# A hash-bucketed attention and two MoE blocks on one core: the order of the attention's queues, chosen anew

## The chip, the cores and the metric

The kernel runs on one core of a Trainium2 chip. The metric is the device time of one execution in microseconds; before the change the median of three runs is 786.19. The engines are TensorE (PE, with its weight loads as PEld), VectorE (DVE), ScalarE (ACT), GpSimd (POOL) and SyncE (SP), which issues all DMAs. Each engine works through its own queue in the order of the program, and an instruction that waits holds all that stand behind it.

## The reference

Sixteen heads (2 batches of 8) of 768 positions and width 64, then two feed-forward blocks over the 1536 tokens of width 512. Cut to what matters:

```python
q_bits = (einsum('bhsd,dk->bhsk', q, proj) > 0)           # six bits; k_bits likewise
mask = bucket(q_bits)[:, :, :, None] == bucket(k_bits)[:, :, None, :]
scores = where(mask, scale * q @ k.T, -1e9)
attn = exp(scores - max(scores)); attn = attn / (sum(attn) + 1e-9)
x = (attn @ v)                                            # [1536, 512]
h = x @ w_in; g = (a0 + a1*h + a2*h2 + a3*h3) / (1 + |b0||h| + |b1|h2 + 1e-6); x = g @ w_out
h = x @ w_in2; out = (h - tanh(h)) @ w_out2
```

## The kernel before

The attention goes head by head, and the heads overlap. For each head h, `load_qk` fetches keys and queries (`kq`), `split_hi` (ScalarE) and `split_lo` (GpSimd) make a rounded part `A` and a rest `Bl`, and `place` copies them by DMA into the operand tiles `TA`, `TBk` and `TBq`. `bits` multiplies with the projection on TensorE, and VectorE turns the signs into mask rows of `TBk` (L361). `smax` (L376) makes the masks' products and VectorE takes each row's maximum `mx` (L380), six blocks j of 128 positions to a head; `put_max` transposes the maxima on TensorE (`mt`, L391), and VectorE makes `mr` of them (L396), which goes to a row of `TBq` by DMA. `scores` (L498) then makes the block `st` of scores, ScalarE its exponential `e` (L501); the exponential is rounded to `eh` by ScalarE (L507), in blocks 2 and 4 partly by VectorE (L509), GpSimd makes the rest `el` (L518), and `attend` multiplies both with V into `pv` (18 small matmuls to a block).

V is read once for a pair of heads (`vraw`). Its scale is a chain through two engines: `vmax` (VectorE, `vm`, L420), `vall` (transpose on TensorE, L429), `vback` (VectorE, L433 and L434, the last writes `vdg`), `vagain` (TensorE, L437) and `vscale` (VectorE, L447 to L450, writes `vsc`). With it `vhi` (ScalarE, L469) and `vlo` (VectorE, L473) write the two halves of the tile `VB`; `vmean_of` (L480) sums over V on TensorE, and ScalarE and VectorE bring that to `VM` (L485, L486). `normalize` (VectorE, L549 to L552) and `to_x` (TensorE transposes, `xh` on ScalarE, `xl` on VectorE, L576) end a pair of heads.

PSUM is shared out in three double banks "d" (for `sm`, `st`, `bits`, `xT`, and the first MoE products `hr`), taken in turn, and one single bank "s" for `mt`, `vt` and the sum over V. A matmul into "d" waits for whoever read the tile three places earlier.

The order is written by hand, by a table. Each step is put on a list with a place: the head's number times six plus an entry of the table `T` (or of `EARLY` for heads 0 to 3, or `T_LAST`), and the list is sorted:

```python
on(g + j, scores, h, j)
on(g + j + T["exp"], out_of, "e", (h, j))
on(g + j + T["round"], round_e, h, j)
on(g + T["vlo"], vlo, h)
...
for _, _, fn, args in sorted(tasks, key=lambda x: x[:2]):
    fn(*args)
```

So a number of the table has no time of its own: it only decides what stands ahead of what on each engine. `EH_ACT_LAST` and `EL_DVE_LAST` say how much of the last head's rounding each engine does. Behind the attention stand the two MoE blocks, whose order is another table, `M`.

Of the kernel before, what the change touches and what calls it, by code (L numbers as in the profile page):

```python
# [38 lines left out]


T = dict(load=-22.01, hi=-15.34, lo=-14.2, place=-13.97, place_a=-13.59, bits=-13.42, bits_out=-12.57,
         put=-3.25, put_out=-3.12, vhi=-6.87, vlo=-4.93, vmean=-2.03, vmean_out=-1.18, lead=9.98, max=0.3,
         exp=0.13, round=0.9, rest=1.95, pv=(5.43, 6.95, 7.43, 8.75, 8.06, 9.23), pv_last=(5.5, 5.5, 7.19,
         8.17, 8.91, 9.32), norm=9.74, x=14.29, x_out=15.02, v=-16.67, vmax=-11.5, vall=-10.2, vscale=-9.9,
         w=-24, w_step=3.88, h0=0.75, slot=0.88, a=0.84, b=2.13, c=2.55, d=4.03, e=4.18, gates=26.99,
         vback=-10.1, vagain=-9.93, w2=-8.0, w2_step=4.0, w_load=6.0)
EARLY = {0: dict(load=-61, hi=-59.04, lo=-59.03, place=-57.89, bits=-57.11, bits_out=-56.82, place_a=-56.45,
                lead=54.43, put=-49.1, v=-59.99, vmax=-57.43, vall=-55.7, vscale=-55.6, vhi=-4.1, vlo=-4.02,
                vmean=-2.21, vmean_out=-1.2, vback=-55.67, vagain=-55.64, put_half=-51.0),
         1: dict(load=-66.5, hi=-64.64, lo=-64.4, place=-61.82, bits=-59.23, bits_out=-58.61, place_a=-57.18,  # L50
                lead=53.53),
         2: dict(load=-64.71, hi=-60, lo=-59.75, place=-59.59, place_a=-59.53, bits=-56.42, bits_out=-56.02,
                lead=9.98, v=-22.32),
         3: dict(load=-20, hi=-15.31, lo=-14.17, place=-14.21, place_a=-13.68, bits=-12.43, bits_out=-11.41,
                lead=9.23)}
NE = 1
T_LAST = dict(norm=9.59, x=10.17, x_out=10.68)
# [3 lines left out]
def tile_fn(ctx: ExitStack, tc: tile.TileContext, kq, v, proj, w1i, w1o, a_, b_, w2i, w2o, out):  # L61
# [180 lines left out]
    with ExitStack() as actx:  # L242
# [354 lines left out]
        for h in range(BH):  # L597
            g, last = 6 * h, h == BH - 1
            T = {**TT, **EARLY.get(h, {})}
            if h > 0:  # L600
# [190 lines left out]
```

## Time and profile before

| | |
|---|---|
| median of three runs | 786.19 us (782.45 to 789.70) |
| profiled execution | 783.02 us, span 781.2 us |
| TensorE busy in the span | 745.8 us (95%) |
| VectorE, ScalarE, GpSimd busy | 525.8, 466.2, 507.0 us (67%, 60%, 65%) |
| attention | up to some 264 us of the span |
| MoE blocks | from there to the end |

A row of the time line names the start in us from the span's start, the duration, the engine, the line of the program, the operation and its operands, and in brackets how long the engine stood idle just before and who ended that. Buffer numbers are left out of the names, so `mx` is the tile of any head.

### The profile page before, as it was taken

How to read it: one execution, taken by the hardware profiler on the slowest of the kernel's cores; microseconds unless marked ns; L12 is line 12 of the kernel's file. 1: busy time of each engine (PE TensorE's matmuls, PEld its weight loads, DVE VectorE, ACT ScalarE, POOL GpSimd, SP SyncE). 2: the span in 40 equal slices, each digit the busy share in tenths (PEclk: the TensorE clock that was granted, in tenths of full speed). 3: DMA queues.
4: the chain of work that ended last, by engine and by line, in shares of the span. 5: the costliest groups of instructions: out<-in, count | busy, mean ns of one | idle time of the engine just before them, and what ended most of it. 6: DMA issues, size and time to landing. Idle time of an engine off the chain costs nothing.

```text
span 781.2 us, 13222 instructions
## 1 busy us (share of the span) xinstructions
PE 745.8 (95%) x5081; PEld 627.9 (80%) x5081; DVE 525.8 (67%) x820; ACT 466.2 (60%) x756; POOL 507.0 (65%) x395
## 2 busy tenths in 40 slices
PE   4799999999899699999999999999999999999998
PEld 3689888888787588888888888888888888888886
DVE  6678988898879888879899898853322444342222
ACT  2388888878796788777666676764444333332120
POOL 2298898988889687787777778985333434342221
PEclk9999999999999999999999999999999999999999
DMA  6564546447421231121222211221221212200012
GB/s 169 159 164 129 136 135 166 127 112 193 119 77 61 62 101 55 55 80 56 59 76 76 61 54 56 74 86 55 71 64 55 82 54 60 77 27 1 28 41 95
DMA packets 40536, 66.49 MB, mean 85 GB/s; under 512 B 3844, under 2 KB 26468, under 8 KB 40472
## 3 DMA queue, kind: packets, MB, share of 16 engines
q1 hardware_dynamic: 40472, 65.63, 28.8%
q8 instruction: 40, 0.66, 0.4%
q14 instruction: 24, 0.20, 0.1%
HBM read 43.00 MB, written 3.15 MB: 59 GB/s over the span
## 4 chain that ended last, share of the span: by engine, by line
PE 82%; DVE 12%; ACT 2%; issue 2%; DMA 1%; SPq 0%; ACTq 0%; DVEq 0%
PE h L171 32%; PE y L691 17%; PE y L687 17%; PE st L498 6%; DVE mx L380 4%; PE sm L376 3%; PE bits L352 2%; DVE eh L509 1%; PE pv L536 1%; DVE VB L473 1%; PE pv L537 1%; PE pv L539 1%; DVE TBk L361 1%; ACT e L501 1%; DMA vraw<-in_v_dram 1%
## 5 line engine op out<-in xcount | busy, mean ns | idle before, releaser
L239 POOL TENSOR_TENSOR G<-g,G 128x512 fp32r<-128x512 f32 x96 | 123.4, 1295 | 119.5 <-ACT G L234 104.6
L518 POOL TENSOR_TENSOR el<-e,eh 128x768 f16<-128x768 f32 (+2 forms) x96 | 159.1, 1673 | 33.0 <-ACT eh L507 20.2
L171 PE MATMUL h<-xh,wh 128*128 128x512 f32 x368 | 144.0, 391 | 3.6 <-DVE wt L110 3.6
L171 PE MATMUL h<-xl,wh 128*128 128x512 f32 x368 | 143.7, 390 | 0.0
L171 PE MATMUL h<-xh,wl 128*128 128x512 f32 x368 | 143.7, 390 | 0.0
L122 POOL TENSOR_TENSOR wl<-wt,wh 128x512 fp32r<-128x512 f32 x64 | 83.6, 1306 | 71.7 <-ACT wh L121 71.1
L687 PE MATMUL y<-G,wh 128*128 128x512 f32 x384 | 118.3, 389 | 0.0
L691 PE MATMUL y<-wh,G 128*128 128x512 f32 x384 | 118.1, 389 | 0.0
L234 ACT CAST G<-g 128x512 fp32r<-128x512 f32 x96 | 58.3, 619 | 84.9 <-PE y L691 35.7
L501 ACT ACTIVATE e<-st,lnk 128x768 f32<-128x768 f32 x96 | 86.2, 899 | 31.7 <-PE st L498 28.3
L110 DVE SCALAR_TENSOR_TENSOR wt<-wt,low 128x512 int32<-128x512 int32 x64 | 44.0, 687 | 89.5 <-ACT wt L98 85.2
L704 DVE TENSOR_TENSOR ya<-y,ya 128x512 f32<-128x512 f32 x72 | 49.1, 688 | 77.8 <-PE y L691 72.7
L380 DVE TENSOR_REDUCE mx<-sm 128x1 f32<-128x768 f32 x96 | 90.7, 951 | 12.7 <-PE sm L376 10.7
L171 PEld LDWEIGHTS h<-xh,wh 128*128 128x128 f32 x368 | 69.5, 189 | 18.2 <-issue 3.8
L691 PEld LDWEIGHTS y<-wh,G 128*128 128x128 f32 x384 | 72.1, 188 | 14.9
L687 PEld LDWEIGHTS y<-G,wh 128*128 128x128 f32 x384 | 72.1, 188 | 14.9
L209 ACT ACTIVATE s<-h 128x512 f32<-128x512 f32 x48 | 28.5, 598 | 90.4 <-PE h L171 90.3
L171 PEld LDWEIGHTS h<-xh,wl 128*128 128x128 f32 x368 | 69.4, 188 | 14.6
L171 PEld LDWEIGHTS h<-xl,wh 128*128 128x128 f32 x368 | 69.5, 189 | 14.4
L691 PE MATMUL y<-wl,G 128*128 128x512 f32 x192 | 74.7, 389 | 0.0
L687 PE MATMUL y<-G,wl 128*128 128x512 f32 x192 | 74.7, 389 | 0.0
L507 ACT CAST eh<-e 128x768 f16<-128x768 f32 (+2 forms) x92 | 68.1, 740 | 1.5
(122 smaller groups left out, 1603.2 us busy)
## 6 DMA issues: line engine op xcount, KB each, us to landing
raw<-in_w1i_dram SPq DMA_DIRECT2D x16, 512.0 KB
raw<-in_w1o_dram SPq DMA_DIRECT2D x16, 512.0 KB
raw<-in_w2i_dram SPq DMA_DIRECT2D x16, 512.0 KB
raw<-in_w2o_dram SPq DMA_DIRECT2D x16, 512.0 KB
kq<-in_kq_dram SPq DMA_DIRECT2D x16, 384.0 KB
TA<-A SPq DMA_DIRECT2D x32, 192.0 KB
TA<-Bl SPq DMA_DIRECT2D x32, 192.0 KB
vraw<-in_v_dram SPq DMA_DIRECT2D x8, 384.0 KB
```

The lines of the kernel that those rows point to most:

```text
L122: lo_eng.tensor_sub(lo, w, hi)
L171: nc.tensor.matmul(ps, l[:, dc], r[:, dc], start=(n == 0), stop=(n == 11))
L234: nc.scalar.copy(gh, live[u, fi])
L239: nc.gpsimd.tensor_sub(gl, live.pop((u, fi)), gt[u, fi])
L380: d = nc.vector.tensor_reduce(mx[h][:, j:j + 1], ps, axis=AX.XY, op=ALU.max)
L498: nc.tensor.matmul(ps[:, n], l[h][0:k, j * P:(j + 1) * P], q[h][0:k, n * SH:(n + 1) * SH], start=(k == P), stop=(k < P))
L501: outs["e", (h, j)] = lambda: nc.scalar.activation(halved(e), ps, AF.Exp, scale=1.0 / math.sqrt(D), bias=lnk)
L507: nc.scalar.copy(eh[h, j][:, 0:n], ef[h, j][:, 0:n])
L518: nc.gpsimd.tensor_sub(el[h, j][:, n:S], e[:, n:S], eh[h, j][:, n:S])
L687: nc.tensor.matmul(ps, l[:, o], r, start=(n == 0), stop=(n == 11))
L691: nc.tensor.matmul(ps, l[:, o], r, start=(n == 0), stop=(n == 11))
L704: nc.vector.tensor_add(ya, ps, ya)
```

## The change

Only the tables `T` and `EARLY` have other numbers. `M`, `T_LAST`, `EH_ACT_LAST` and `EL_DVE_LAST` are as they were. The core of the diff:

```diff
-         put=-3.25, put_out=-3.12, vhi=-6.87, vlo=-4.93, vmean=-2.03, vmean_out=-1.18, lead=9.98, max=0.3,
-         exp=0.13, round=0.9, rest=1.95, pv=(5.43, 6.95, 7.43, 8.75, 8.06, 9.23), pv_last=(5.5, 5.5, 7.19,
...
+         put=-3.25, put_out=-3.08, vhi=-6.87, vlo=-3.9, vmean=-1.86, vmean_out=-0.71, lead=9.98, max=0.3,
+         exp=0.42, round=0.9, rest=1.95, pv=(5.43, 6.95, 7.92, 8.75, 8.16, 9.23), pv_last=(5.5, 5.5, 7.99,
```

VectorE's queue in the middle of the attention, where heads 8 and 9 overlap; `mx9` are maxima of head 9, `vt5`, `vdg5` and `vsc5` the scale of the sixth pair, `VB0` the low half of V for head 9. Before:

```order
L380 TENSOR_REDUCE mx9_2173<-sm9_4_2374 128x1
L420 TENSOR_REDUCE vm5_2379<-vraw5_2141 128x2
L473 SCALAR_TENSOR_TENSOR VB0_124<-vraw4_1599,vsc4_1933,VB0_124 128x6x64
L380 TENSOR_REDUCE mx9_2173<-sm9_5_2409 128x1
L433 TENSOR_REDUCE vt5_2433<-vt5_2433 2x1
L434 TENSOR_TENSOR vdg5_2435<-ident_64,vt5_2433 2x2
L447 TENSOR_SCALAR vt5_2433<-vt5_2433 128x2
L448 TENSOR_SCALAR vt5_2433<-vt5_2433 128x2
L450 RECIPROCAL vsc5_2475<-vt5_2433 128x2
L380 TENSOR_REDUCE mx10_2450<-sm10_0_2451 128x1
L396 TENSOR_SCALAR mr9_0_2502<-mt9_0_2500 6x128
L509 CAST eh8_2_2505<-e8_2_2444 128x384
```

And with the change:

```order
L420 TENSOR_REDUCE vm5_2377<-vraw5_2139 128x2
L380 TENSOR_REDUCE mx9_2172<-sm9_4_2374 128x1
L380 TENSOR_REDUCE mx9_2172<-sm9_5_2409 128x1
L433 TENSOR_REDUCE vt5_2412<-vt5_2412 2x1
L434 TENSOR_TENSOR vdg5_2414<-ident_64,vt5_2412 2x2
L473 SCALAR_TENSOR_TENSOR VB0_124<-vraw4_1597,vsc4_1915,VB0_124 128x6x64
L447 TENSOR_SCALAR vt5_2412<-vt5_2412 128x2
L448 TENSOR_SCALAR vt5_2412<-vt5_2412 128x2
L450 RECIPROCAL vsc5_2457<-vt5_2412 128x2
L380 TENSOR_REDUCE mx10_2449<-sm10_0_2450 128x1
L509 CAST eh8_2_2502<-e8_2_2443 128x384
L396 TENSOR_SCALAR mr9_0_2505<-mt9_0_2500 6x128
```

`vm5` has gone ahead of a maximum, `VB0` from ahead of `vdg5` to behind it, and the cast of `eh8_2` ahead of `mr9`. The last of these moves is there in every head.

ScalarE's queue at the end of head 8 (`e8_4` and `e8_5` are exponentials, `VB1` the high half of V for head 10, `VM0` the sum over V of head 9). Before:

```order
L501 ACTIVATE e8_4_2561<-st8_4_2562,lnk_70 128x768
L485 ACTIVATE VM0_134<-vm9_2548 64x64
L507 CAST eh8_4_2590<-e8_4_2561 128x512
L501 ACTIVATE e8_5_2595<-st8_5_2596,lnk_70 128x768
L469 ACTIVATE VB1_125<-vraw5_2141,vsc5_2475 128x6x64
```

And with the change:

```order
L501 ACTIVATE e8_4_2548<-st8_4_2549,lnk_70 128x768
L507 CAST eh8_4_2588<-e8_4_2548 128x512
L469 ACTIVATE VB1_125<-vraw5_2139,vsc5_2457 128x6x64
L485 ACTIVATE VM0_134<-vm9_2562 64x64
L501 ACTIVATE e8_5_2593<-st8_5_2594,lnk_70 128x768
```

`VM0` has gone behind `eh8_4`, and `VB1` ahead of `e8_5`. VectorE's part of `VM` (L486) has gone behind its cast of `eh` in block 4 likewise.

SP's queue at the start of the program, before:

```order
L280 DMA kq0_96<-in_kq_dram 128x768
L286 DMA praw_95<-in_proj_dram 128x6
L280 DMA kq1_140<-in_kq_dram 128x768
L415 DMA vraw0_142<-in_v_dram 128x6x128
L335 DMA TBk0_153<-A0_144 64x768
L336 DMA TBq0_154<-A0_144 64x768
L342 DMA TA0_152<-A0_144 64x768 x2
L342 DMA TA0_152<-Bl0_145 64x768 x2
L335 DMA TBk1_173<-A1_148 64x768
```

And with the change:

```order
L280 DMA kq0_96<-in_kq_dram 128x768
L286 DMA praw_95<-in_proj_dram 128x6
L415 DMA vraw0_140<-in_v_dram 128x6x128
L280 DMA kq1_142<-in_kq_dram 128x768
L335 DMA TBk0_153<-A0_144 64x768
L336 DMA TBq0_154<-A0_144 64x768
L335 DMA TBk1_169<-A1_148 64x768
L336 DMA TBq1_170<-A1_148 64x768
L342 DMA TA0_152<-A0_144 64x768 x2
L342 DMA TA0_152<-Bl0_145 64x768 x2
```

`vraw0` has gone ahead of `kq1`, and the copies of head 1's `A1` ahead of four copies of head 0. On TensorE, `vall` and `vagain` of most pairs have each gone ahead of one block of pv, and the sum over V (L480) behind the next scores or `smax`; the first `smax` of head 1 stands ahead of the second half put of head 0, and in the last head the product `hr0_1` stands ahead of a pv block.

## Rows read from the trace of the kernel before

**Rows 1.** Stretches: start and end, length, busy us and instructions by engine, TensorE's granted clock, DMA

```profile
130.00:157.00 27.00, 25.74 (x349) 23.04 (x347) 23.52 (x39) 22.19 (x32) 23.75 (x15) 1.00 0.51 136
184.00:211.00 27.00, 24.13 (x286) 20.13 (x286) 24.21 (x39) 20.12 (x30) 21.65 (x15) 0.94 0.57 148
...
264.00:510.00 246.00, 245.51 (x1077) 203.23 (x1078) 214.65 (x322) 175.64 (x302) 195.12 (x171) 0.99 0.22 69
```

**Rows 2.** TensorE's waits from 50 to 186 us: total, times, longest

```profile
PE vt L437 <- DVE vdg L434: 3.5, 4, 0.9
PE bits L352 <- DVE mx L380: 0.7, 3, 0.3
...
PEld sm L376 <- DVE xl L576: 0.8, 2, 0.4
```

**Rows 3.** Time line of VectorE around the scale of a pair

```profile
137.55 0.96 DVE L380 TENSOR_REDUCE mx<-sm 128x1 f32<-128x768 f32 x1
...
139.41 1.67 DVE L473 SCALAR_TENSOR_TENSOR VB<-vraw,vsc,VB 128x384 f16<-128x384 f32 x1
141.01 0.94 DVE L380 TENSOR_REDUCE mx<-sm 128x1 f32<-128x768 f32 x1
...
142.19 0.14 DVE L434 TENSOR_TENSOR vdg<-ident,vt 2x2 f32<-2x2 f32 x1
142.80 0.17 DVE L447 TENSOR_SCALAR vt<-vt 128x2 int32<-128x2 int32 x1 [0.47 <-PE vt L437]
...
143.21 0.17 DVE L450 RECIPROCAL vsc<-vt 128x2 f32<-128x2 f32 x1
```

**Rows 4.** Time line of TensorE at the same place

```profile
142.39 0.38 PE L437 MATMUL vt<-vdg,pj 2*128 2x2 f32 x2 [0.94 <-DVE vdg L434]
...
143.43 0.27 PE L391 MATMUL mt<-ident,mx 128*6 128x128 f32 x1
```

**Rows 5.** Instructions on VB, 30 to 240 us: shortest, median, longest in ns

```profile
L473 DVE SCALAR_TENSOR_TENSOR VB<-vraw,vsc,VB x15: 610/1228/1858, 32.9 to 223.5; 128x384 f16<-128x384 f32 x15
```

**Rows 6.** Time line of GpSimd over two heads

```profile
137.34 5.25 POOL L518 TENSOR_TENSOR el<-e,eh 128x768 f16<-128x768 f32 x3 [0.22 <-ACT eh L507]
...
150.92 5.19 POOL L518 TENSOR_TENSOR el<-e,eh 128x768 f16<-128x768 f32 x3 [0.71 <-ACT eh L507]
156.08 1.83 POOL L327 TENSOR_TENSOR Bl<-kq,A 128x768 fp32r<-128x768 f32 x1
```

**Rows 7.** Time line of VectorE, the head behind

```profile
147.85 0.22 DVE L486 SCALAR_TENSOR_TENSOR VM<-vm,VM 32x64 f16<-32x64 f32 x1
...
148.95 0.96 DVE L380 TENSOR_REDUCE mx<-sm 128x1 f32<-128x768 f32 x1 [0.55 <-PE sm L376]
...
156.31 0.28 DVE L396 TENSOR_SCALAR mr<-mt 6x128 fp32r<-6x128 f32 x1 [0.97 <-PE mt L391]
156.51 1.62 DVE L509 CAST eh<-e 128x384 f16<-128x384 f32 x1
```

**Rows 8.** Time line of VectorE at the start

```profile
7.93 0.95 DVE L420 TENSOR_REDUCE vm<-vraw 128x2 f32<-128x768 f32 x1 [1.68 <-DMA vraw<-in_v_dram]
...
22.13 3.55 DVE L380 TENSOR_REDUCE mx<-sm 128x1 f32<-128x768 f32 x4 [0.54 <-PE sm L376]
```

**Rows 9.** Time line of ScalarE at the start, the second split

```profile
5.78 0.83 ACT L323 CAST A<-kq 128x768 fp32r<-128x768 f32 x1 [1.14 <-DMA kq<-in_kq_dram]
```

**Rows 10.** Time line of ScalarE around the fifth and sixth exponential of a head

```profile
146.58 0.90 ACT L501 ACTIVATE e<-st,lnk 128x768 f32<-128x768 f32 x1 [0.31 <-POOL el L518]
147.38 0.20 ACT L485 ACTIVATE VM<-vm 64x64 f16<-64x64 f32 x1
147.51 0.62 ACT L507 CAST eh<-e 128x512 f16<-128x512 f32 x1
148.66 0.90 ACT L501 ACTIVATE e<-st,lnk 128x768 f32<-128x768 f32 x1 [0.53 <-PE st L498]
149.46 0.61 ACT L469 ACTIVATE VB<-vraw,vsc 128x384 f16<-128x384 f32 x1
```

More of the change, by code (lines that the diff above doesn't have):

```diff
@@ L41 @@
 T = dict(load=-22.01, hi=-15.34, lo=-14.2, place=-13.97, place_a=-13.59, bits=-13.42, bits_out=-12.57,
-         put=-3.25, put_out=-3.12, vhi=-6.87, vlo=-4.93, vmean=-2.03, vmean_out=-1.18, lead=9.98, max=0.3,
-         exp=0.13, round=0.9, rest=1.95, pv=(5.43, 6.95, 7.43, 8.75, 8.06, 9.23), pv_last=(5.5, 5.5, 7.19,
-         8.17, 8.91, 9.32), norm=9.74, x=14.29, x_out=15.02, v=-16.67, vmax=-11.5, vall=-10.2, vscale=-9.9,
-         w=-24, w_step=3.88, h0=0.75, slot=0.88, a=0.84, b=2.13, c=2.55, d=4.03, e=4.18, gates=26.99,
@@ L46 @@
[L46 to L51, printed above, removed]
+         put=-3.25, put_out=-3.08, vhi=-6.87, vlo=-3.9, vmean=-1.86, vmean_out=-0.71, lead=9.98, max=0.3,
@@ new lines @@
+         exp=0.42, round=0.9, rest=1.95, pv=(5.43, 6.95, 7.92, 8.75, 8.16, 9.23), pv_last=(5.5, 5.5, 7.99,
+         8.17, 8.91, 9.32), norm=9.74, x=14.29, x_out=15.02, v=-16.67, vmax=-11.73, vall=-10.86,
+         vscale=-9.9, w=-24, w_step=3.88, h0=0.84, slot=0.88, a=0.84, b=1.9, c=2.55, d=4.03, e=4.18,
+         gates=25.39, vback=-10.1, vagain=-9.93, w2=-8.0, w2_step=4.0, w_load=6.0)
+EARLY = {0: dict(load=-60.86, hi=-59.04, lo=-58.85, place=-57.89, bits=-56.87, bits_out=-56.82, place_a=-55.78,
+                lead=54.43, put=-48.95, v=-60.87, vmax=-57.43, vall=-55.7, vscale=-55.6, vhi=-4.1,
+                vlo=-4.02, vmean=-2.21, vmean_out=-0.98, vback=-55.67, vagain=-55.64, put_half=-51.0),
+         1: dict(load=-66.2, hi=-64.64, lo=-64.4, place=-61.82, bits=-58.5, bits_out=-58.21, place_a=-57.18,
+                lead=54.99),
@@ L52 @@
          2: dict(load=-64.71, hi=-60, lo=-59.75, place=-59.59, place_a=-59.53, bits=-56.42, bits_out=-56.02,
-                lead=9.98, v=-22.32),
-         3: dict(load=-20, hi=-15.31, lo=-14.17, place=-14.21, place_a=-13.68, bits=-12.43, bits_out=-11.41,
+                lead=9.66, v=-22.32),
+         3: dict(load=-20, hi=-15.99, lo=-14.17, place=-14.21, place_a=-13.68, bits=-12.43, bits_out=-11.41,
                 lead=9.23)}
```

## The prediction

> **What bounds the kernel now.** I read the stretches first, then TensorE's waits, then the order of time on the engines that TensorE waits for. The profiled execution took 783.0 us, of which its span is 781.2. In the stretches [rows 1] the reader is to see two kernels in one. In the MoE stretch TensorE is busy for 245.51 of 246 us: nothing is to be won there, and the change doesn't touch it. In a stretch of two heads of the attention it is busy for 25.74 of 27 us, and VectorE, ScalarE and GpSimd for 23.52, 22.19 and 23.75. So the attention runs at TensorE's pace, with some 1.3 us of TensorE's waits in each pair of heads, and the other engines have only 3 to 5 us of rest there. In 184 to 211 us, where the MoE weights join, TensorE idles for 2.9 us and its mean granted clock is 0.94. The question is how many of TensorE's waits ahead of the MoE stage a new order takes away.
>
> The waits name their causes [rows 2]. Over the heads that run from 50 to 186 us, TensorE stood 3.5 us in four waits for `vdg`, the little tile that VectorE makes between `vall` and `vagain` of a pair of heads; 0.7 us in three waits of `bits` for a row maximum; and its weight loads 0.8 us in two waits of `smax` for `xl`. That is 5.0 us. All are waits for VectorE, which works strictly in its order, so a shuffle of VectorE's queue can have a price.
>
> **The change part by part.** No instruction is added, taken away or given to another engine; the lists of before and after hold the same rows in another order. The tables that split a rounding (EH_ACT_LAST, EL_DVE_LAST) stand as they were, so the "other split of the last head's rounding" has no price: no such instruction differs. POOL's queue is the same row for row.
>
> *Part 1, the chain of a pair's scale (four pairs).* Before, in time [rows 3]: a maximum at 137.55, `vm` behind it, `VB` at 139.41 for 1.67 us, the last maximum at 141.01, `vdg` from 142.19 to 142.33, 0.47 us of wait for TensorE's `vagain`, and `vsc` from 143.21 to 143.38. TensorE's `vagain` went at 142.39 after 0.94 us of wait, and the transpose `mt` at 143.43, right behind `vsc`, since both use the single PSUM bank "s" [rows 4]. After: `vm`, two maxima, `vdg`, and only then `VB` and `vsc`. From 137.55 to 142.33 are 4.78 us; without `VB`, which holds the queue from 139.41 to 141.01, they are 3.18, and `vdg` is there at 140.7. On TensorE `vagain` now stands one block of pv earlier, near that time, so its wait almost goes. But now `VB` stands between `vdg` and `vsc`, and TensorE can't pass `mt` before `vsc`. `VB` lasts from 0.61 to 1.86 us [rows 5]; the long ones end with a GpSimd instruction. At 137.34 GpSimd began three `el` that took 5.25 us together [rows 6], so the second ended at 140.84, and the `VB` of 139.41 ended at 141.08, 0.24 behind it. After the change `vsc` ends at 140.7 + 0.61 + 0.58 = 141.9 if GpSimd leaves `VB` alone, and at 140.7 + 1.86 + 0.58 = 143.2 if it meets a whole `el`. (0.58 is from `vscale`'s first start to its last end, 142.80 to 143.38.) Against 143.38 the gain is 1.5 at best, of which TensorE can use its own 0.9, and 0.2 at worst. I take 0.35, nearer to the bad end, since GpSimd is busy for 23.75 of 27 us. Four pairs: 1.4 us, bounds 0.8 and 3.5.
>
> The Trainium skill (SBUF — State Buffer, section "Who interferes with whom") says that a VectorE instruction with two SBUF inputs is fully blocked until the GpSimd instruction that came first has ended. The trace has only 0.24 us from that end to the end of `VB`, though a `VB` alone takes 0.61. By the rule taken literally `VB`, and `vsc` with it, would come 0.37 later in each pair, and this part would give nothing; the sum goes by the row.
>
> *Part 2, the rounding of e_2 ahead of the put of the maxima (three pairs).* Before, `mr` waited 0.97 us for TensorE until 156.31, and the cast of `eh` behind it began at 156.51 and lasted 1.62 us [rows 7], because GpSimd's `Bl` had begun at 156.08 for 1.83 us [rows 6]. `xl` and the maximum that `bits` waits for stand behind it. After, the cast stands ahead of `mr`: it can begin at 156.31 - 0.97 = 155.34, meets the `el` that ends at 156.08, and should end near 156.3; `mr` follows, to 156.6. VectorE is through at 156.6 where it was at 158.1. That covers the waits of `bits` and of `smax` for `xl`, 0.7 + 0.8 = 1.5 us in all. `vmean` has moved behind `smax`, which costs nothing: it stands in the wait of `bits`. I take 1.2, bounds 0 and 1.5. The put that `mr` starts is wanted only by the next head's scores.
>
> *Part 3, the start.* `vraw0` is fetched ahead of `kq1`. VectorE waited 1.68 us for it, to 7.93 [rows 8], with the first thresholds queued behind; `kq1`, one place ahead in SP's queue, let ScalarE go at 5.78 [rows 9]. In its place `vraw0` would land near that, so the most is 1.68; the least is 0, if its many short rows rather than its place made it late. I take 1.2. `smax` of head 1 goes ahead of the second half put, which hides up to the 0.54 us at 22.13 [rows 8]; I take 0.3. `kq1` comes later now, and with it `Bl1`, the copies behind it and kq2's load; the work that they feed stands behind the thresholds and six maxima of 0.95, and covers them. If that cover were gone, the start would give 0. Together 1.5, bounds 0 and 2.2.
>
> *Part 4, ScalarE and the last head.* The high half of V goes ahead of e_5, and `VM` behind the cast of `eh`. In front of e_5 ScalarE waited 0.53 us for TensorE, and that is the cover of V's 0.61 us [rows 10]. Price nothing; without the cover it is up to 0.6 per head, since the next head's scores wait for e_5. For `hr0_1`, ahead of a pv block in the last head, I take nothing: the stage behind it waits for VectorE, whose order is unchanged there.
>
> Sum: 1.4 + 1.2 + 1.5 = 4.1 us, so 783.0 - 4.1 = 778.9 for an execution like the profiled one. The median of the three runs is 786.2, some 3 us above the profiled one; against the median the forecast is 782.1, say **782**. The bounds of the parts, 0.8 and 7.2, make 779 to 785.4 of it.
>
> **The rivals.** *Nothing but the start.* `VB` meets GpSimd in every pair for longer than its worst row, and TensorE waits at `mt` for what it no longer waits at `vagain`; part 2's cast meets the next instruction of GpSimd. For it speaks that POOL's queue is unchanged and nearly full; against it, that even the worst `VB` leaves 0.2. Then 1.5 us remain: 784.7. The split that isn't there belongs here too: it adds nothing.
>
> *More than the sum.* All 5.0 us of waits and 2.2 of the start go, and the stretch from 184 to 211 gets back half of its 2.9 us: 5.0 + 2.2 + 1.5 = 8.7, 777.5. Against it speaks that three other engines have so little rest that waits come back elsewhere.
>
> *Slower: VM on the path.* VectorE takes `VM` from ScalarE ahead of the fourth maximum. ScalarE now makes it behind `eh` (0.62) and V (0.61): e_4 ends at 147.48, and `VM`, which was there at 147.58, comes at about 148.8 [rows 10]. VectorE's own part takes 0.22, and the fourth maximum began at 148.95 after 0.55 us of wait for TensorE [rows 7]. So it just fits: from 148.73 on, every lateness goes into the maximum, the thresholds behind it and the next scores. If 13 heads lose 0.6 us there, they lose 7.8, and with the 4.1 gained the time is 789.9. For it speaks the narrow fit; against it, that ScalarE and VectorE come earlier there if parts 1 and 2 hold.
>
> **How the numbers follow.** The forecast has 0.57, the start alone 0.18, more than the sum 0.13, VM on the path 0.12. The range reaches to the rivals on both sides until no more than 2 in 10 are left out: 777 to 788, where the forecast's own is 779 to 785.4. One per cent, 7.9 us, is about what a measurement of this kernel can tell from no change. Below 778.3 lies most of the second rival: faster 0.12. Above 794.1 `VM` would have to cost half as much again: slower 0.04. The rest, 0.84, is no change.
>
> **What would show it.** Part 1 is right if `vagain`'s wait falls from 0.9 to under 0.3 and `mt` takes over less than half of it. Part 2 is right if the waits of `bits` and of `smax` for `xl` are gone and the casts of 1.62 end soon after an `el`. Part 3 is right if `vm` of the first pair begins before 7. The slower rival would show as VectorE's waits at VM for ScalarE. The whole shows in the time at which the MoE stretch begins. What would make the forecast wrong is a wait that I put in another engine's shadow, above all GpSimd meeting VectorE at other places than before.

## The result, and the profile after the change

| | before | after |
|---|---|---|
| median | 784.46 us (8 executions, 782.45 to 789.70) | 777.20 us (8 executions, 774.57 to 779.73) |
| profiled execution | 783.02 us, span 781.2 us | 775.10 us, span 773.3 us |
| first product of the MoE stage | 264.49 us | 255.81 us |

The ratio of after to before is 0.9896, with a 95% interval from 0.9862 to 0.9931: faster by about 1%, some 8 us, where 4 were forecast. The eight executions after lie in two groups, 774.6 to 775.1 us and 779.3 to 779.7 us; the profiled one is of the first, as the profiled one of before is among its fastest. So the traces are compared with each other, and ratios with ratios.

Which stretch gave the time is read from the first pv block of each head. It began earlier than before by 0.8 us in head 0, 1.5 in head 1, 7.1 in head 11, 9.0 in head 15, and the MoE stage by 8.7 us, of which 0.8 was lost again behind it, where TensorE ran at half clock for longer (6.8 us instead of 3.4). The products `hr`, which stand in the last head, are not counted to the MoE stage here. A pair of heads in the middle takes 25.67 us instead of 27.00 (from the pv of head 5 to that of head 11, divided by three).

The stretches of after that answer to [rows 1] (start and end, length, busy us and instructions of TensorE, its weight loads, VectorE, ScalarE and GpSimd, TensorE's granted clock, DMA share and GB/s):

```profile
127.00:154.00 27.00, 26.80 (x356) 24.21 (x357) 24.60 (x42) 23.85 (x35) 25.17 (x15) 1.00 0.52 141
178.00:211.00 33.00, 31.36 (x415) 27.20 (x412) 31.26 (x51) 29.79 (x46) 29.28 (x19) 1.00 0.53 142
256.00:500.00 244.00, 244.00 (x1068) 201.79 (x1069) 212.00 (x318) 174.54 (x299) 194.24 (x170) 0.99 0.22 69
```

TensorE is now idle for 0.2 us in 27 of the middle heads, where it was 1.3, and it has kept full speed up to 211 us, where its mean was 0.94 before. The waits of the middle heads from 50 to 186 us, which answer to [rows 2] (us in total, times, longest):

```profile
PEld vt L437 <- DVE vdg L434: 1.0, 4, 0.2
...
PE st L498 <- DVE mx L380: 0.2, 1, 0.2
```

The 3.5 us of `vdg` are 1.0 us on the weight load alone, which TensorE's other work covers; the waits of `bits` and of `smax` for `xl` are gone. How the scale's chain looks on VectorE (start, duration), beside [rows 3]:

```profile
133.10 0.95 DVE L420 TENSOR_REDUCE vm<-vraw 128x2 f32<-128x768 f32 x1
134.09 1.82 DVE L380 TENSOR_REDUCE mx<-sm 128x1 f32<-128x768 f32 x2
...
136.14 0.14 DVE L434 TENSOR_TENSOR vdg<-ident,vt 2x2 f32<-2x2 f32 x1
136.21 0.60 DVE L473 SCALAR_TENSOR_TENSOR VB<-vraw,vsc,VB 128x384 f16<-128x384 f32 x1
...
137.22 0.17 DVE L450 RECIPROCAL vsc<-vt 128x2 f32<-128x2 f32 x1
```

From the first of these to the end of `vsc` are 4.29 us; before, the same instructions took 5.83, from 137.55 to 143.38. On TensorE, beside [rows 4], `vagain` and `mt` go without a wait in brackets:

```profile
136.40 0.38 PE L437 MATMUL vt<-vdg,pj 2*128 2x2 f32 x2
137.83 0.27 PE L391 MATMUL mt<-ident,mx 128*6 128x128 f32 x1
```

And the instructions on `VB`, beside [rows 5] (count, shortest, median and longest in ns):

```profile
L473 DVE SCALAR_TENSOR_TENSOR VB<-vraw,vsc,VB x15: 601/771/1269, 34.4 to 215.7; 128x384 f16<-128x384 f32 x15
```

The median `VB` fell from 1.23 to 0.77 us, and in the middle heads the `VB` behind `vdg` took 0.60 each time. That is the row on which the forecast failed.

### The profile page after: what moved, and what is told of

Read it like the earlier page. It is cut to its first block, busy times and chain, and to the rows that moved or that the text cites. A ratio compares the mean times of both kernels' runs of the same rounds, so it can differ in the third digit from the quotient of the medians.

```text
span 773.3 us, 13226 instructions
## 1 busy us (share of the span) xinstructions
PE 743.6 (96%) x5081; PEld 626.0 (81%) x5081; DVE 527.3 (68%) x820; ACT 470.2 (61%) x756; POOL 508.4 (66%) x395
## 4 chain that ended last, share of the span: by engine, by line
PE 88%; DVE 8%; ACT 2%; issue 1%; DMA 1%; SPq 0%; DVEq 0%; ACTq 0%
PE h L171 33%; PE y L691 17%; PE y L687 17%; PE st L498 8%; PE sm L376 4%; PE bits L352 3%; DVE mx L380 2%; PE pv L536 2%; PE pv L537 2%; PE pv L539 1%; ACT e L501 1%; DVE eh L509 1%; PE vm L480 1%; DVE el L516 1%; DVE low L108 1%
## 5 line engine op out<-in xcount | busy, mean ns | idle before, releaser
L110 DVE SCALAR_TENSOR_TENSOR wt<-wt,low 128x512 int32<-128x512 int32 x64 | 44.0, 688 | 89.8 <-ACT wt L98 85.3
```

## The experiments

The forecast had four parts. Each was made alone on the kernel before, then undone alone in the changed kernel. The table is read from the traces, a row for each kernel: the first pv block of heads 0, 5, 11 and 15, the mean length of a pair of heads (from head 5 to head 11, divided by three), the first MoE product and TensorE's wait ahead of it, all in us; then the median time and the ratio to the kernel before on the same chip.

| kernel | 0 | 5 | 11 | 15 | pair | MoE | wait | median | ratio (95%) |
|---|---|---|---|---|---|---|---|---|---|
| before | 40.95 | 108.25 | 189.26 | 241.55 | 27.00 | 264.49 | 3.62 | | 1 |
| after | 40.18 | 105.13 | 182.15 | 232.57 | 25.67 | 255.81 | 3.62 | 777.20 | 0.9896 (0.9862 to 0.9931) |
| a1_scale | 42.45 | 109.96 | 188.11 | 241.87 | 26.05 | 267.10 | 5.63 | 784.72 | 0.9969 (0.9945 to 0.9993) |
| a2_cast | 44.37 | 114.56 | 193.41 | 245.19 | 26.28 | 270.44 | 5.65 | 789.18 | 1.0020 (0.9991 to 1.0049) |
| a3_start | 40.39 | 108.03 | 189.04 | 241.93 | 27.00 | 268.46 | 7.76 | 789.29 | 1.0033 (1.0005 to 1.0062) |
| a4_mean | 41.21 | 110.56 | 191.41 | 242.65 | 26.95 | 270.02 | 7.77 | 791.61 | 1.0054 (1.0026 to 1.0082) |
| c1_no_scale | 38.78 | 106.99 | 187.32 | 238.69 | 26.78 | 261.92 | 3.62 | 783.03 | 0.9953 (0.9929 to 0.9977) |
| c1_vb_back | 40.60 | 108.24 | 189.49 | 240.89 | 27.08 | 264.11 | 3.61 | 785.76 | 0.9973 (0.9949 to 0.9997) |
| c2_no_cast | 42.24 | 109.37 | 187.30 | 236.28 | 25.98 | 259.51 | 3.62 | 776.21 | 0.9878 (0.9841 to 0.9916) |
| c3_start_back | 42.72 | 107.68 | 184.69 | 239.07 | 25.67 | 260.90 | 3.55 | 778.39 | 0.9897 (0.9873 to 0.9920) |
| c4_no_mean | 41.98 | 108.50 | 183.42 | 234.71 | 24.97 | 257.92 | 3.62 | 778.47 | 0.9902 (0.9866 to 0.9939) |
| v_behind | 42.44 | 112.38 | 192.53 | 247.27 | 26.72 | 270.27 | 3.55 | 785.49 | 0.9995 (0.9971 to 1.0018) |
| before_free | 40.39 | 107.97 | 189.52 | 243.30 | 27.18 | 262.40 | 0 | 782.05 | 0.9942 (0.9918 to 0.9966) |
| after_free | 39.91 | 104.89 | 181.87 | 232.27 | 25.66 | 251.62 | 0 | 773.66 | 0.9847 (0.9797 to 0.9897) |
| f_start | 43.85 | 110.81 | 187.79 | 240.51 | 25.66 | 259.45 | 0 | 777.82 | 0.9883 (0.9851 to 0.9914) |
| f_mean | 41.72 | 106.40 | 181.34 | 232.31 | 24.98 | 251.65 | 0 | 773.35 | 0.9827 (0.9793 to 0.9862) |
| f_mix2 | 41.15 | 104.86 | 179.86 | 230.83 | 25.00 | 250.19 | 0 | 771.40 | 0.9818 (0.9789 to 0.9846) |

### Each part alone

**a1_scale**, part 1 alone:

```diff
-vlo=-4.93, pv=(5.43, 6.95, 7.43, 8.75, 8.06, 9.23), vmax=-11.5, vall=-10.2
+vlo=-3.9, pv=(5.43, 6.95, 7.92, 8.75, 8.16, 9.23), vmax=-11.73, vall=-10.86
```

> The kernel before with part 1 alone: in every second head vm and vdg ahead of the maxima and of VB, VB behind vdg, TensorE's vagain one block of pv earlier. Theory 'each part pays by itself': VB costs 0.6 to 0.8 us, since it begins where GpSimd changes from one instruction to the next; the waits for vdg go, 0.9 to 1.0 us for each pair from the third head on, so the MoE stage begins 4 to 6 us earlier than before (at 258.5 to 260.5) and the time falls by as much. Rival 'only together': VB costs 1.2 us or more, TensorE waits at mt for vsc instead, and the gain stays under 2 us (MoE stage at 262.5 or later).

**a2_cast**, part 2 alone:

```diff
-put_out=-3.12
+put_out=-3.08
```

> The kernel before with part 2 alone: the cast of eh_2 ahead of mr. Theory 'each part pays by itself': the waits of bits and of smax for xl go, about 0.3 us a pair, 1 to 1.5 us in all (MoE stage at 263.0 to 263.5); the waits for vdg stay at 3 us or more. Rival 'only together': the cast still meets a GpSimd instruction and lasts 1.6 us, or the time saved goes into the unchanged wait for vdg: under 0.5 us.

**a3_start**, part 3 alone: the whole table `EARLY` of the changed kernel with the table `T` of before.

> The kernel before with the start's numbers alone (vraw0 ahead of kq1, smax of head 1 ahead of the second half put). Theory 'each part pays by itself': 0.8 us at the first pv, as in the changed kernel, and the same 0.8 at the MoE stage (263.7). Rival 'the waits behind take it back': vm still begins by 6.4 us, but the first heads wait for something else and the MoE stage begins within 0.3 us of before.

**a4_mean**, part 4 without the last head:

```diff
-exp=0.13, vmean=-2.03, vmean_out=-1.18
+exp=0.42, vmean=-1.86, vmean_out=-0.71
```

> The kernel before with ScalarE's part alone: the high half of V ahead of e_5, VM behind the cast of eh_4, the mean's matmuls one place later. Theory 'each part pays by itself': no change, within 0.5 us either way (MoE stage at 264.0 to 265.0). Rival 'VM on the path': VectorE waits at VM for ScalarE and the time rises by 2 us or more. Rival 'a hidden share': it gives 1 us or more by itself, which parts 1 and 2 were taken to give.

In the middle heads part 1 shortens a pair by 0.95 us, as the first theory had it, and part 2 by 0.72, where it had 0.3; the start and ScalarE's part shorten it by nothing. But the times are another story. Part 1 gave 0.3% where its pairs alone are worth 4 to 5 us, and parts 3 and 4 were slower than before. Both theories missed that. With parts 1 and 2 some of it was lost ahead of the first pv block, 1.5 and 3.4 us later than before; the column of waits shows another part, and with parts 3 and 4 most of it: ahead of the first MoE product TensorE stood 3.62 us before and after, 5.6 with part 1 or 2 alone, and 7.8 with part 3 or 4 alone. The transposes and the first product of a3_start:

```profile
259.82 0.87 PE L568 MATMUL xT<-ident,xt 128*128 128x128 f32 x6 [1.42 <-DVE g L226]
...
268.46 0.80 PE L171 MATMUL h<-xh,wh 128*128 128x512 f32 x1 [7.76 <-DVE g L226]
```

and of the changed kernel:

```profile
251.31 0.88 PE L568 MATMUL xT<-ident,xt 128*128 128x128 f32 x6 [1.44 <-DVE g L226]
...
255.81 0.77 PE L171 MATMUL h<-xh,wh 128*128 128x512 f32 x1 [3.62 <-DVE wt L110]
```

The product is the same; what releases it differs. Its PSUM bank is one that an attention tile had. In the kernel before and in the changed one that tile's last reader is VectorE's `wt` (L110), in a1_scale and a2_cast the `g` (L226) of the third of the products `hr`, in a3_start and a4_mean that of the fourth, each 2.1 us further down VectorE's queue. The three double buffers of the attention take turns, and a shuffle anywhere in it can change which of them ends where. The change as a whole happens to leave this as it was.

### What the first MoE product waits for

**after_free** is the changed kernel and **before_free** the kernel before, both with the three PSUM pools of the attention laid out in another order, so that the first MoE product inherits the bank of pv:

```diff
-pvp = ...; dbl = ...; sgl = ...
+dbl = ...; sgl = ...; pvp = ...
```

> The changed kernel with the attention's three PSUM pools laid out in another order (the double buffers, the bank 's', then pv's), nothing else. In the alone-runs the first MoE product waited for the last reader of the bank that it inherits: 3.6 us behind the last transpose where that is VectorE's low, 5.6 and 7.8 us where it is g of the router products 2 and 3. Here it inherits pv's bank, which is free by then, and waits only for xl. Theory 'the bank is what it waits for': the wait ahead of the first MoE product falls from 3.6 to 2.0 to 2.2 us, the second product may wait instead for low, which the first one's 2.7 us cover; the time falls by 1.4 to 3 us below the changed kernel's 777.2 (the half clock that follows the wait may be shorter too). Rival 'it waits for the weights or the rounding instead': within 0.5 us of the changed kernel.

> The kernel before with the other order of the PSUM pools, nothing else. Theory 'the bank's wait is independent of the attention's order': the wait of 3.6 us ahead of the first MoE product goes, as it did in the changed kernel, and the time falls by 3 to 5 us, to 781.5 to 783.5. Rival 'half clock and other lateness take its place': less than 2 us.

The wait went altogether, not to 2 us: the `xl` that the product reads had been made long before. After_free on TensorE:

```profile
250.99 0.88 PE L568 MATMUL xT<-ident,xt 128*128 128x128 f32 x6 [1.44 <-DVE g L226]
251.62 0.48 PE L171 MATMUL h<-xh,wh 128*128 128x512 f32 x1
...
255.48 0.47 PE L171 MATMUL h<-xh,wh 128*128 128x512 f32 x1 [0.86 <-DVE wt L110]
```

The first product begins right behind the transposes, and the second waits 0.86 us for what the first had waited for. The time fell by 0.5% of before with either order of the attention (0.9896 to 0.9847, and 1 to 0.9942), 4 to 4.5 us. So the bank's wait is a cost of its own and not a part of what the change brought: with the bank out of the way the change is worth 0.9942 - 0.9847, again 1%. The other experiments keep the bank of the changed kernel (c1, c2, c3, c4, v_behind) or leave it free (f_start, f_mean, f_mix2).

### One part undone

**c1_no_scale**, **c1_vb_back** (of part 1 the place of `VB` alone), **c2_no_cast** and **c4_no_mean** are the changed kernel with these numbers back:

```diff
 c1_no_scale: vmax=-11.5, vall=-10.2, vlo=-4.93, pv=(5.43, 6.95, 7.43, 8.75, 8.06, 9.23)
 c1_vb_back:  vlo=-4.93
 c2_no_cast:  put_out=-3.12
 c4_no_mean:  exp=0.13, vmean=-2.03, vmean_out=-1.18
```

> The changed kernel with part 1 undone: vm, vdg, VB and vagain stand where they stood before; the first MoE product still inherits the PSUM bank that VectorE's low frees. Theory 'two kinds of wait under one floor' (TensorE's own work in a pair of heads is about 25.65 us; part 1 takes 0.95 a pair away, part 2 0.8, and together they can't give more than the 1.3 that there were): a pair takes 26.2 us, as with part 2 alone, so the MoE stage begins 2.5 to 3.5 us later than in the changed kernel (258.3 to 259.5) and the time is about 3 us above it. Rival 'only together': the whole 1.3 a pair comes back, 27.0 us, and the MoE stage begins after 262.

> The changed kernel with VB alone put back: the low half of V ahead of vdg again, vm and the maxima and vagain stay where the change has them. Theory 'VB's place is what part 1 wins': TensorE waits 0.6 to 1.0 us for vdg in each pair again, a pair takes 26.3 to 26.7 us and the time rises by 3.5 to 6 us above the changed kernel (781 to 784). Rival 'vm and the maxima are what it wins': a pair stays at 26.0 us or less and the time at 779.5 or less.

Without part 1 a pair takes 26.78 us and the ratio is 0.9953: the part is worth 1.0 to 1.1 us a pair, 4.5 us in all (0.0057 of 786). The theory had 26.2, the rival 27.0: parts 1 and 2 win nearly in full beside each other, and don't share one floor. With `VB` alone put back (one maximum earlier in every head, and so ahead of `vdg` in every second) a pair takes 27.08 and the ratio is 0.9973: 6 us, by its interval no less than the whole part, so what part 1 wins is the place of `VB`. TensorE's waits of c1_vb_back from 50 to 186 us:

```profile
PE vt L437 <- DVE vdg L434: 6.1, 4, 1.5
```

Four waits of 1.5 us, longer than the 0.9 of before, since `vagain` now stands one block of pv earlier. The chain on VectorE:

```profile
139.46 1.72 DVE L473 SCALAR_TENSOR_TENSOR VB<-vraw,vsc,VB 128x384 f16<-128x384 f32 x1
141.11 0.94 DVE L380 TENSOR_REDUCE mx<-sm 128x1 f32<-128x768 f32 x1
...
142.28 0.14 DVE L434 TENSOR_TENSOR vdg<-ident,vt 2x2 f32<-2x2 f32 x1
```

and the `el` that `VB` met on GpSimd:

```profile
139.12 1.65 POOL L518 TENSOR_TENSOR el<-e,eh 128x768 f16<-128x768 f32 x1 [0.37 <-ACT eh L507]
```

> The changed kernel with part 2 undone: the cast of eh_2 behind mr again; the first MoE product's bank as in the changed kernel. Theory 'two kinds of wait under one floor': a pair takes 26.0 us, as with part 1 alone, waits of bits of 0.25 come back once a pair, the MoE stage begins 1.5 to 2.5 us later than in the changed kernel (257.3 to 258.3). Rival 'only together': 26.6 us a pair or more, MoE stage after 260.5.

A pair takes 25.98 us, 0.3 more than in the changed kernel, by five waits of 0.2 us of `smax` for `xl`; those of `bits` did not come back. Over the five pairs from head 1 to head 11 that is 1.5 us by the rows. The measured ratio, 0.9878, is no higher than the changed kernel's, so the time doesn't show it.

> The changed kernel with ScalarE's part undone: V's high half behind e_5, VM ahead of eh_4 and the mean's matmuls one place earlier; the first MoE product's bank as in the changed kernel. Theory 'it costs and gives nothing in the steady heads': a pair stays at 25.7 us, the MoE stage within 1 us of the changed kernel. Rival 'it makes room for part 2': with VM ahead of eh_4 the cast and the maxima come late again and a pair takes 26.0 us or more.

Neither theory: a pair became shorter, 24.97 us, while the time stayed (0.9902 to 0.9896). More of this part below.

### Where VB meets GpSimd

**v_behind** is the changed kernel with `VB` behind `vsc` in every second head, past the three small instructions that stand between:

```diff
-vlo=-3.9
+vlo=-3.85
```

> The changed kernel with VB moved two places further in every second head, behind the copy of vt and vsc, nothing else. In the changed kernel VB begins 0.06 us ahead of the end of a GpSimd el and takes 0.60, and the next el takes 2.01 where one alone takes 1.65. Theory 'the place in GpSimd's row sets VB's price': here VB begins about 0.6 us later, some 0.5 into the next el, and lasts 1.2 to 1.6 us; that el is back at 1.65. VB stands in no one's way up to vsc, so TensorE's waits for vdg and mt stay away, the maxima come 0.6 to 1.0 later, and a pair takes 25.7 to 26.4 us. Rival 'VB costs 0.6 wherever it stands behind vdg': VB 0.60 to 0.65, the pair at 25.67.

VectorE of v_behind at the place:

```profile
144.55 0.14 DVE L434 TENSOR_TENSOR vdg<-ident,vt 2x2 f32<-2x2 f32 x1
...
145.78 1.03 DVE L473 SCALAR_TENSOR_TENSOR VB<-vraw,vsc,VB 128x384 f16<-128x384 f32 x1
```

GpSimd of v_behind, the `el` that was running:

```profile
144.74 1.65 POOL L518 TENSOR_TENSOR el<-e,eh 128x768 f16<-128x768 f32 x1
```

and the one behind it:

```profile
146.34 2.16 POOL L327 TENSOR_TENSOR Bl<-kq,A 128x768 fp32r<-128x768 f32 x1
```

In the changed kernel GpSimd's two `el` around `VB` were these:

```profile
134.62 1.65 POOL L518 TENSOR_TENSOR el<-e,eh 128x768 f16<-128x768 f32 x1 [0.36 <-ACT eh L507]
```

```profile
136.33 2.00 POOL L518 TENSOR_TENSOR el<-e,eh 128x768 f16<-128x768 f32 x1
```

So `VB` has no price of its own. In c1_vb_back it began 1.31 us ahead of the end of an `el` and ended 0.41 behind it (141.18 to 140.77). In v_behind it began 0.61 ahead and ended 0.42 behind (146.81 to 146.39). In the changed kernel it began 0.06 ahead and took its own 0.60. That agrees with the first theory in kind, and the size that it gave, 1.2 to 1.6, was too high: a meeting costs what is left of the `el` and 0.41 us more, or 0.60 if that is longer. Over all 17 traces, each of the 162 `VB` that began 0.2 us or more ahead of the end of a GpSimd instruction ended 0.42 us behind that end. The boundary is narrow, though. In f_mix2, further down, a `VB` began 0.07 us ahead of the end of one `el`, much as in the changed kernel; but the next `el` began 0.04 us behind the start of `VB`, where it was 0.12 there, and went ahead of it:

```profile
199.82 2.11 DVE L473 SCALAR_TENSOR_TENSOR VB<-vraw,vsc,VB 128x384 f16<-128x384 f32 x1
```

```profile
198.25 3.26 POOL L518 TENSOR_TENSOR el<-e,eh 128x768 f16<-128x768 f32 x2
```

It ended 0.42 us behind the second `el` (201.93 to 201.51). F_mean has such a `VB` too; the changed kernel has none.

The GpSimd instruction behind it pays too: 2.00 where an `el` alone takes 1.65, 2.16 where `Bl` took 1.83 [rows 6]. Moving this one instruction past three small ones, in every second head, cost the whole gain: a pair of 26.72 us, where 25.7 to 26.4 were expected, and a ratio of 0.9995. TensorE did not wait for `vdg` there, as expected, but at `smax`, once for the copy of the thresholds and three times for ScalarE:

```profile
PE sm L376 <- DMA TBq<-TBk: 1.5, 1, 1.5
PE sm L376 <- ACT eh L507: 1.5, 2, 0.9
PE sm L376 <- ACT e L501: 1.0, 1, 1.0
```

How 0.4 us on VectorE and 0.33 on GpSimd become 1 us a pair I did not resolve.

The Trainium skill (SBUF — State Buffer, section "Who interferes with whom") says that whichever of the two engines issues first holds the shared ports for its whole instruction, and that the order of issue decides which one pays. By that rule, the trace agrees in the order: `VB` pays where it comes second, the next `el` where `VB` is under way. In the size it differs: a `VB` fully blocked until the `el` ended would end 0.60 behind it, and the rows have 0.41 and 0.42.

### The start

**f_start** is after_free with the table `EARLY` of before. **c3_start_back** is the changed kernel with that table but for `lead=9.66` of head 2, which keeps the MoE product's bank.

> The changed kernel with the other order of the PSUM pools and with the start's numbers of before. Compared with the same order of pools and the changed start. Theory 'the start keeps what it gives': the first pv comes 0.6 to 1.5 us later and the MoE stage as much later, time 774 to 776. Rival 'the heads behind take it back' (the start alone left 0.2 us at head 11): MoE stage within 0.5 us, time within 1 us of 773.7, once stretches at half clock are set aside.

> The changed kernel with the start's numbers of before but for one (head 2's lead), which leaves the first MoE product's PSUM bank as in the changed kernel: kq1 ahead of vraw0, mt ahead of the first scores of head 1. Theory 'the start gives what the forecast took' (1.5 us; over the profiles so far the first pv begins at 42.2 on the mean of six with the old start and 40.7 on the mean of eight with the new): time 1 to 2.5 us above the changed kernel (778.7 to 780.3). Rival 'the clock takes it back' (TensorE runs the first heads at half clock up to 31 to 46 us whatever the order): within 0.7 us.

In c3_start_back `vm` waits for its data again as in [rows 8], 1.53 us to 7.61, and the first pv block begins at 42.72 instead of 40.18. The ratios are 0.9897 and 0.9896, with intervals of 0.24% and 0.35% on either side: the time shows no gain, and could not show one below some 3 us. F_start was slower than after_free by 2.8 us as ratios (the medians, from two chips, lie 4 us apart), more than expected, but the second MoE product waited 2 us longer in it, so not all of that is the start. Over all traces the first pv block begins at 42.28 on the mean of seven with the old start and 40.94 on the mean of ten with the new: 1.3 us, in a spread of 2 us on either side. That spread goes with the clock, though the column of the granted clock is misleading here. The stretches of the changed kernel at the start

```profile
8.00:18.00 10.00, 6.03 (x22) 5.42 (x22) 7.97 (x14) 1.38 (x2) 1.80 (x1) 1.00 0.67 173
18.00:28.00 10.00, 7.25 (x24) 5.11 (x25) 8.55 (x11) 0.80 (x2) 1.81 (x1) 0.51 0.76 191
28.00:38.00 10.00, 9.63 (x39) 8.03 (x37) 5.63 (x12) 7.77 (x11) 5.71 (x4) 0.50 0.35 121
```

beside one of f_mix2, with the same start

```profile
28.00:38.00 10.00, 9.22 (x38) 8.06 (x37) 5.22 (x12) 7.36 (x11) 5.68 (x4) 1.00 0.35 121
```

show 0.50 and 1.00 of the clock at the same place. But the matmuls of the scores take the same time there (count, shortest, median and longest in ns; the changed kernel, then f_mix2), and f_mix2's own take a third less from 43 us on:

```profile
L498 PE MATMUL st<-TA x10: 522/522/668, 28.4 to 37.1; 128*128 128x384 f32 x10
```

```profile
L498 PE MATMUL st<-TA x10: 522/522/669, 28.4 to 37.5; 128*128 128x384 f32 x10
...
L498 PE MATMUL st<-TA x10: 332/338/442, 43.0 to 51.1; 128*128 128x384 f32 x10
```

So both ran at half clock, 1.2 GHz: the trace of f_mix2 has no record of the clock ahead of 40.3 us, and a stretch without one is printed as 1.00. Read this way, TensorE rose to full speed, to keep it for over 45 us, at 31.5 to 46.2 us in the 17 traces. A straight line through them, an estimate, has the first pv block 0.27 us later for each us that this is later; with that taken out, the new start is 1.36 us earlier than the old (95%: 0.8 to 1.9). So the start's 1.3 us stand by the rows and are not shown in the times.

### VM's place, and a faster kernel

**f_mean** is after_free with the place of `VM` and of the mean's matmuls as before; **f_mix2** has them as before from the fourth head on, and at the changed place in heads 1 and 2:

```diff
 f_mean and f_mix2: T:
-vmean=-1.86, vmean_out=-0.71
+vmean=-2.03, vmean_out=-1.18
 f_mix2 alone: EARLY[1] and EARLY[2]:
+vmean=-1.86, vmean_out=-0.71
```

> The changed kernel with the other order of the PSUM pools, and with VM and the mean's matmuls back where they stood before; V's high half stays ahead of e_5. With both of these undone a pair took 24.97 us where the changed kernel takes 25.67. Theory 'VM's place costs 0.7 us a pair in the steady heads and pays in the first five heads': a pair takes 25.0 to 25.2 us, the first five heads 1 to 1.6 us more, time within 1.5 us of 773.7. Rival 'it is V's high half': a pair stays at 25.6 us or more. Rival 'a better kernel': the steady heads' gain stays, 771.5 us or less.

> The changed kernel with the other order of the PSUM pools and with VM and the mean's matmuls back at their places of before from the third head pair on, but at the changed places in the first heads. Theory 'VM's new place pays in the first heads and costs 0.7 us a pair behind them': TensorE's waits of 0.96 us at the mean and 1.1 us at sm between 36 and 57 us go, a pair takes 25.0 us, the MoE stage begins at 249 to 250 and the time is 770 to 772. Rival 'the waits in the first heads come from the clock, not from VM's place': as with VM back everywhere, 773.3, within 1 us.

A pair takes 24.98 and 25.00 us, so 0.7 us a pair is the price of the new place of `VM` and the mean's matmuls, which these runs move together; V's high half stands in the changed place in both and costs nothing. A stretch of the middle heads in f_mix2:

```profile
100.00:125.00 25.00, 25.00 (x349) 23.22 (x349) 22.91 (x39) 22.48 (x32) 23.72 (x15) 1.00 0.56 147
```

TensorE is busy for all of it. GpSimd and TensorE in the changed kernel, 100 to 180 us (waited for, total, times, longest):

```profile
POOL el L518 <- ACT eh L507: 2.6, 6, 0.6
...
PEld st L498 <- ACT e L501: 1.0, 4, 0.3
...
POOL el L518 <- ACT VM L485: 1.0, 3, 0.3
```

With `VM` and V behind `eh`, ScalarE is late with e_5 and with the next `eh`; GpSimd waits for it, and TensorE's weight loads wait for `e`. In f_mean GpSimd's waits for `eh` of ScalarE are 0.9 us in three, and TensorE has none for `e`. The loads' 1.0 us in four waits are less than half of the 2.1 us that three pairs lose. The rest is no idle time of TensorE: from head 5 to head 11 its gaps add up to 0.13 us a pair, against none in f_mean. By the start times 0.3 to 0.4 us a pair lie between the last matmul of a pv block and the scores behind it; how much is `VM`'s and how much the mean's I did not separate. In the first heads the new place does pay: f_mean waits 1.0 us at the mean and 1.1 at `smax` between 36 and 57 us, and f_mix2 does not. F_mix2 keeps both. It is the fastest kernel of the study, 771.40 us, 1.8% below before, and its interval doesn't touch that of the changed kernel.

## Why the prediction was wrong

The forecast took the right direction and half of the size: 4.1 us by its sum, 782 us, against 777.2. The time is that of the rival "More than the sum", and the reason is mostly that rival's too: all but 0.2 us of TensorE's waits in the middle heads went, while of its 2.2 us at the start 0.8 came.

*Part 1 is the term that was mis-sized.* Forecast 1.4 us, 0.35 a pair, bounds 0.8 to 3.5; undone it measures 4.5 us, 1.1 a pair, and `VB` put back 6. Two steps failed. The first is "I take 0.35, nearer to the bad end, since GpSimd is busy for 23.75 of 27 us". A busy share doesn't tell where in the other engine's row an instruction falls. The two queues are locked to each other by the heads, so `VB` falls on the same place in every pair of the middle heads, and it fell on a boundary: it took 0.60 each time, `vsc` came 1.54 us earlier, the best end of the range (1.5), and `mt` took over nothing. The test named in the forecast, that `mt` should take over less than half of the wait, came out at none. The second is the count. "Four pairs" were the waits of 0.9 us in a window; the gain runs over the five pairs between head 1 and head 11 and on into heads 12 and 13.

The row behind it was misread too. The forecast put the end of the `el` at 140.84 by dividing three into equal parts and found `VB` 0.24 us behind. Seen by itself on GpSimd of the kernel before, the `el` is this:

```profile
139.01 1.66 POOL L518 TENSOR_TENSOR el<-e,eh 128x768 f16<-128x768 f32 x1
```

It ended at 140.67, and `VB` at 141.08, 0.41 behind, which is the number that v_behind and c1_vb_back give. With it the worst meeting would have cost 2.06, not 1.86, and the 0.37 us that the forecast works out beside it would be 0.19; the bounds were no better than the reading.

*Part 2 was right in size by the rows, but by luck.* Forecast 1.2; undoing it costs 0.3 us a pair, 1.5 over five pairs, and the waits named in the forecast went. The cast takes 0.92 us where it took 1.62 [rows 7], and `mr` follows it. In the changed kernel, on VectorE:

```profile
149.98 0.92 DVE L509 CAST eh<-e 128x384 f16<-128x384 f32 x1
151.03 0.28 DVE L396 TENSOR_SCALAR mr<-mt 6x128 fp32r<-6x128 f32 x1
```

In the time this part could not be seen. Without part 4 it gives far more than the forecast had, 0.72 a pair alone and 1.08 beside part 1 (26.05 in a1_scale, 24.97 in c4_no_mean); part 4 takes most of that back. Parts 1 and 2 do add: 0.95 and 0.72 alone, 2.03 together.

*Part 3 was right by the rows and open in the time.* `vm` began at 6.32, below the 7 that the forecast named, and the first pv block comes 1.3 to 1.4 us earlier over all traces, against 1.5. On VectorE of the changed kernel:

```profile
6.32 0.95 DVE L420 TENSOR_REDUCE vm<-vraw 128x2 f32<-128x768 f32 x1
```

The forecast left out that these heads run at half clock up to a point that differs from trace to trace, which moves the block by more than the term.

*Part 4 was wrong.* Price "nothing", with 0.6 us a head if the cover were gone. The cover of V's high half held. `VM` and the mean's matmuls cost 0.7 us in each pair of the middle heads, some 3 us in all, and paid about 1 us in the first ones (from head 0 to head 5: 63.71 us in f_mix2, 64.68 in f_mean). The mechanism is in part that of the rival "Slower: VM on the path", at 0.35 us a head instead of 0.6, and by another road: not as VectorE's wait at `VM` (0.2 us, once), but as GpSimd's and TensorE's for ScalarE behind it. And a cover was gone, one that the forecast names under part 2: the mean's matmuls cost nothing behind `smax` since there they stand "in the wait of `bits`", a wait that the same lines count as won. The table bears out that it hangs on part 2. With the cast in its old place part 4 costs a pair nothing (27.00 to 26.95; 26.05 in a1_scale, 25.98 in c2_no_cast), with the cast ahead of `mr` it costs 0.50 (26.28 in a2_cast, 26.78 in c1_no_scale) and 0.70 (24.97 in c4_no_mean, 25.67); the start, which the c kernels have besides, changes no pair. That the cover was the wait of `bits`, and no other that the cast's move takes away, no run shows by itself.

*The stretch behind* (184 to 211 us) gave 1.9 us from head 11 to head 15, where the sum had none and the rival 1.5. Heads 12 and 13 gained 3.0, among it the half clock at 206 to 209 us that was not entered; head 14 gave 1.65 back, in a wait of 1.79 us for a maximum.

So the 8.7 us at the MoE stage are 0.8 at the start, 0.7 in heads 0 and 1, 5.6 in five pairs of 1.1, 1.9 in the last heads, and -0.3 behind them. The new numbers of the last head were not made alone, and what they give or cost stays open. The five pairs are the surplus: 5.6 us where parts 1 and 2 had 2.6 together. The rivals "Nothing but the start" and "Slower" did not come. The range held the time by 0.2 us, and the chance of 0.12 for a gain of over 1% was too low for a kernel whose middle stretch had a plain 1.3 us of waits a pair and a change that reordered the engine that all of them waited for.

## What to carry to other kernels

When an instruction is moved to where it may meet another engine's, don't price the meeting by that engine's busy share: in a periodic schedule it is the same meeting every time, so lay the two rows side by side at the new time and take the price that this place has, or name both ends and let them carry equal chances. If the place is a boundary, ask how narrow it is. A move that costs nothing because somebody waits there must be priced again if the same change takes that wait away. And ask which on-chip buffers the next stage inherits: a shuffle far upstream can change which buffer that is, and here that was worth 2 to 4 us by itself, up to half of what the change brought.

## What the runs showed of the hardware

- A VectorE instruction with two SBUF inputs that meets a GpSimd one ends 0.41 to 0.42 us behind it, whether it had waited 1.31 or 0.61 us, though alone it takes 0.60. The GpSimd instruction that follows took 0.33 and 0.35 us longer in the two cases shown.
- Ahead of the MoE stage, the twelve traces in which TensorE waited 3.5 us or more for the first product all fell to half clock there, for 3.4 to 10.2 us; the five in which it did not wait had none there. The changed kernel and f_mix2:

```profile
254.00:261.00 7.00, 5.19 (x13) 4.16 (x14) 6.72 (x11) 3.22 (x6) 5.20 (x5) 0.53 0.24 75
```

```profile
250.00:257.00 7.00, 6.15 (x29) 4.80 (x28) 6.29 (x11) 4.82 (x10) 5.68 (x6) 1.00 0.26 75
```

- At the start TensorE ran at half clock, its matmuls of the scores taking 0.52 us each instead of 0.34, up to 38.7 us in the changed kernel (but for 3.4 us from 14.8 on) and up to 40.3 in f_mix2; over the 17 traces full speed came, to last, at 31.5 to 46.2 us. With one trace for each kernel, they don't show whether the kernel or the execution decides that. In the ten traces with the new start the first pv block lies between 38.8 and 42.4 us, a spread larger than the start's own term.
